# Loads of q and v put behind a product's copy on GpSimd, and the first weights and products of an attention-and-MoE kernel set in another order

## The chip, the cores and the metric

The kernel runs on one core of a Trainium2 chip. The metric is the device time of one launch in microseconds (us), lower is better. Engines are named as the profile names them: PE is TensorE's matrix unit, DVE is VectorE, ACT is ScalarE, POOL is GpSimd, and SP is SyncE, which here only issues DMAs.

## The reference

The program chains three layers. The MoE weights are stored in 64-bit floats, which the kernel reads as pairs of 32-bit words.

```python
# attention: q, k, v are 4 x 8 x 768 x 64; mem_k, mem_v are 4 x 8 x 8 x 64
for c in range(nc):                       # 24 chunks of 32 queries
    l_start = max(0, c_start - 16); r_end = min(S, c_end + 8)
    k_full = concatenate([mem_k, k[:, :, l_start:r_end]], axis=2)
    v_full = concatenate([mem_v, v[:, :, l_start:r_end]], axis=2)
    scores = matmul(q_c, k_full.T) / sqrt(64)
    a = exp(scores - max(scores)); a = a / (sum(a) + 1e-09)
    out[:, :, c_start:c_end] = matmul(a, v_full)
x = out.transpose(0, 2, 1, 3).reshape(3072, 512)
# MoE 1
h = x @ w_in                              # 512 x 2048
x = (h * tanh(log1p(exp(h)))) @ w_out     # 2048 x 512
# MoE 2
h = x @ w2_in
return (h / (1 + exp(-1.702 * h))) @ w2_out
```

## The kernel before, in words

The 3072 tokens are cut into 8 blocks of 384 (`TB`). Attention of a block works on four pairs of heads (hp 0 to 3). The first product of MoE 1 (x times w_in) for a block is 16 products, one for each 128 columns of w_in; they are numbered f0 to f15 within a block and `i = 16 j + f` over the program. All of them are `forward(j, f)`, whose matmuls stand on line 1166. In block 0 a product is 4 plain float32 matmuls, one for each pair of heads' 128 rows of x; from block 1 on it is 12 matmuls on high and low parts. Attention of block j+1 is woven between the products of block j: its scores (L1003), transposes of the exponentials (L1045) and values (L1065) on PE, its maxima (L1018), norms (L1037) and the transposes of loaded q (L679) and k (L682) on DVE, its exponentials (L1025) on ACT. It comes in two sets of two pairs of heads per block. Block 0's own attention stands ahead of everything and has its own code: exponentials L877, norms L896 and L904, transposes L923, values L940, copies of x L975 and L977. The layers behind (the second product of MoE 1 and both of MoE 2) run from about 370 us on and are not touched.

Each product's result leaves PSUM by a copy on ACT (L1298) or DVE (L1299) into a tile `z`, `gl` or `ev`, and goes from there to DRAM.

A tile W of w_in (W0 to W15, one per product) is loaded as 512 KB of 64-bit words by SP and converted in four steps: a drop (L423 on ACT; it could also be DVE), a shift (L432), a low part (L436) and a sign (L440) on DVE. From block 1 on the products use high and low parts made of it (L536 on ACT, L541 on DVE).

The order on each engine is not written by hand. Every operation is handed to a planner (`Plan`) with a rank, its engine's cost and the buffers that it reads and writes; `issue()` goes through them with assumed costs and lags and sets one static order per engine, in which each engine then runs. A buffer made by `fixed()` has no tile behind it: an operation that reads it is placed behind the writer in the plan, and no semaphore comes of it on the chip. Three such buffers matter here. `pace[i]` is written by product i. `opened` is written by a POOL copy of one element of block 0's values (`junk`, L1115), behind which v of block 1 is issued. `passed(j, i)` returns `pace[i]` for blocks from 2 on, so that loads of q and k stand `AHEADK` = 8 product ranks and those of v `AHEADV` = 4 ranks behind in the plan alone.

`load` (L382) issues DMAs: on SP, or on POOL when `via` is set. Loads of q of blocks 2 on and of v of blocks 1 on go through POOL; k always through SP. POOL and SP work through their queues in order, so a DMA issue that has to wait holds those behind it.

```python
load(rank - (LEAD if j == 1 and hp < 2 else 4), ql, qs, P * TB * 4, 128, passed(j, rank - AHEADK), via=NARROW * (j > 1))
load(rank, vt, parts, P * NCH * D * 4, 256, opened if j == 1 else passed(j, rank - AHEADV), via=NARROW)
```

Of the kernel before, what the change touches and what calls it, by code (L numbers as in the profile page):

```python
# [9 lines left out]
F32 = mybir.dt.float32  # L10
# [5 lines left out]
DRAM = bass.MemoryType.DRAM  # L16

NEG = -3.0e38
WARM = 11
NARROW = 0.64  # L20
WIDE = 0.95
# [1 line left out]
HELD = 4  # L23
LEAD = -1
AHEADW = 8
AHEADV = 4
SOON = 4
AHEAD = 6
CUT = 6
# [42 lines left out]
def fixed(t=None):  # L72

    b = Buf(None, None, None)
    b.tile = t
    return b
# [234 lines left out]
def kernel(  # L311
# [139 lines left out]
    def w_first(f):  # L451
        if f % 2 == 0:
            pairs.append(T[f"wo{f // 2}"].new([P, 2 * DM], F32))
        wi[f] = Part(pairs[-1], f % 2 * DM, DM)
        w_conv(1, f, 0, f - 1.5, (), wi[f], f"wi{f}")

    def w_cut(f):
        v = wi[f]
# [141 lines left out]
            tensor=src.tensor, offset=src.offset + r0 * D + col, ap=[[st * D, n] for st, n in dims] + [[1, width]]  # L600
        )

    x0, mem_t, pace, started, opened = {}, {}, {}, [], []

    class Inputs:

# [37 lines left out]
    def passed(j, i):  # L644
        return [pace[i]] if j > 1 and i >= 0 else []

    def pair_of_heads(j, hp, rank):
        b, s0 = divmod(j * TB, S)
        ql = T["ql"].new([P, TB // 32, 32], F32)
        kl = T["kl"].new([P, NKB, 32], F32)  # L650
        qT = T["qT"].new([P, 2 * (GQ + P)], F32)
        kT = T["kT"].new([P, NKB, BLK], F32)
        qs, ks = [], []
        for hh in range(2):
            for e in range(2):
                p0 = (2 * hh + e) * 32
                r0 = (b * H + 2 * hp + hh) * S + s0
                qs.append(lambda p0=p0, r0=r0, e=e: (
                    ql[p0:p0 + 32], rows(q, r0, [(1, 32), (32, TB // 32)], e * 32, 32)
                ))  # L660

                parts = [(0, 32, 0, NKB, -LEFT)]
                if r0 == 0:
                    parts = [
                        (0, 32, 1, NKB - 1, 32 - LEFT), (LEFT, 32 - LEFT, 0, 1, 0), (0, LEFT, 0, 1, 0)
                    ]
                elif r0 + TB == B * H * S:
                    parts = [
                        (0, 32, 0, NKB - 1, -LEFT), (0, LEFT, NKB - 1, 1, TB - LEFT),
                        (LEFT, 32 - LEFT, NKB - 1, 1, TB - LEFT),  # L670
                    ]
                for row, n, c, nb, t in parts:
                    ks.append(lambda row=row, n=n, c=c, nb=nb, t=t, p0=p0, r0=r0, e=e: (
                        kl[p0 + row:p0 + row + n, c:c + nb, :],
                        rows(k, r0 + t, [(1, n), (32, nb)], e * 32, 32),
                    ))
        load(rank - (LEAD if j == 1 and hp < 2 else 4), ql, qs, P * TB * 4, 128, passed(j, rank - AHEADK), via=NARROW * (j > 1))
        load(rank - (LEAD if j == 1 and hp < 2 else 4), kl, ks, P * NKB * 128, 128, passed(j, rank - AHEADK))
        add(rank, [("dve", dve(TB), lambda: nc.vector.transpose(  # L679
            out=qT[:, :TB], in_=ql.get().rearrange("p c d -> p (c d)")  # L680
        ))], reads=[ql], writes=[qT])
        add(rank, [("dve", dve(NKB * CHUNK), lambda: nc.vector.transpose(out=kT[:, :, :CHUNK], in_=kl.get()))], reads=[kl], writes=[kT])  # L682
        whole = fixed()

        def memory(eng):
            eng.tensor_copy(
                out=kT[:, :NCH, CHUNK:],
                in_=mem_t[b][:, hp, 0:NM].unsqueeze(1).to_broadcast([P, NCH, NM]),
            )

        add(
            rank,
            [("dve", dve(NCH * NM), lambda: memory(nc.vector)), ("pool", 0.3, lambda: memory(nc.gpsimd))],
            reads=[mem_t[b], kT], writes=[whole],
        )
        return qT, kT, whole

    def values_of(j, h0, rank):

        b, s0 = divmod(j * TB, S)  # L700
        vt = T["vh"].new([P, NCH, D], F32)
        parts = []
        for i in range(2):
            h = b * H + h0 + 2 * i
            t = h * S + s0 - LEFT
            runs = [(0, CHUNK, t, 0, NCH), (BLK, KEYS - BLK, t + CHUNK, 0, NCH)]
            if (h + 1) * S == B * H * S and s0 + TB == S:
                runs[1:] = [
                    (BLK, KEYS - BLK, t + CHUNK, 0, NCH - 1), (BLK, LEFT, t + TB, NCH - 1, 1),
                    (BLK + LEFT, RIGHT, t + TB, NCH - 1, 1),  # L710
                ]
            for row, n, r0, c, many in runs:
                parts.append(lambda row=i * D + row, n=n, r0=r0, c=c, many=many: (
                    vt[row:row + n, c:c + many], rows(v, r0, [(1, n), (CHUNK, many)], 0, D)
                ))
            if s0 == 0 or j == 1:
                parts.append(lambda row=i * D + CHUNK, h=h: (
                    vt[row:row + NM], rows(mem_v, h * NM, [(1, NM), (0, NCH)], 0, D)
                ))
        load(rank, vt, parts, P * NCH * D * 4, 256, opened if j == 1 else passed(j, rank - AHEADV), via=NARROW)  # L720
        return vt

    def first_values(gp, rank):
# [188 lines left out]
    def quad_out(j, hp, gp, vt, rank, names, e):  # L912
# [56 lines left out]
        for hh in range(1 if apart else 2):  # L969
            part = fixed()  # L970

            def hi(eng, hh=hh):
                x, y = cut(hh, x0[j][0])
                if eng == "act":
                    nc.scalar.activation(out=x, in_=y, func=AF.Copy)  # L975
                else:
                    nc.vector.tensor_copy(out=x, in_=y)  # L977

            def lo(hh=hh):
                x, y = cut(hh, x0[j][1])  # L980
                nc.vector.tensor_tensor(out=x, in0=y, in1=cut(hh, x0[j][0])[0], op=ALU.subtract)

            add(
                rank + 3.4,
                [("act", act(2 * GQ, True), lambda hi=hi: hi("act")), ("dve", dve(2 * GQ), lambda hi=hi: hi("dve"))],
                reads=[o], writes=[x0[j][0].buf(hp), part],
            )
            if j:
                add(rank + 3.6, [("dve", dve(2 * GQ), lo)], reads=[o, part], writes=[x0[j][1].buf(hp)])

    def duo(j, hp0, heads, r0):
# [82 lines left out]
        for i in range(2):  # L1074
# [7 lines left out]
                out=xl.at(hp), in0=o[i].get(), in1=xh.at(hp), op=ALU.subtract))],  # L1082
                reads=[o[i], part], writes=[xl.buf(hp)])

    def quads():

        last, todo = None, []
# [63 lines left out]
    def forward(j, f):  # L1151
# [17 lines left out]
                    n += 1  # L1169

        pace[i] = fixed()
        grain = KD // 2 if j else KD
        for k0 in range(0, KD, grain):
            kks = range(k0, k0 + grain)
            done = [pace[i]] if k0 + grain == KD else []
            add(
                i, [("pe", grain * (3 * 0.174 if j else 0.644), lambda kks=kks: go(kks))],
                reads=[*xs, *ws1], writes=[*done, h],
            )
        if j == 0:  # L1180
            w_cut(f)
        t = T[("gh", "gl", "ev")[i % 3] if j else ("gh", "gl")[f % 2]].new([P, TB], F32)
        copy(i + 0.3 - (URGENT if j else 0), View(t), h)
        (s, th), (fh, p) = divmod(j, 2), divmod(f, NP)
        key = 1, s, 2 * th + fh, p
        gds[key] = fixed()
        load(i + 0.4, gds[key], [lambda: (g1d[2 * th + fh][:, p, s * TB:(s + 1) * TB], t.get())], P * TB * 4, 1536, [t])
# [483 lines left out]
```

## Time and profile before

| what | value |
|---|---|
| median of 3 timed runs | 1097.83 us (1097.22 to 1099.79) |
| time of the profiled execution | 1095.65 us |
| its span in the profile | 1093.9 us |
| TensorE's mean granted clock in it | 0.990 of full speed |
| busy share of the span: PE, DVE, ACT, POOL | 98%, 73%, 49%, 15% |

The first row is what the kernel is judged by. The others come from one execution that was recorded by the profiler; the 1.75 us between its time and its span lie outside what the trace shows. A busy share is a mean over the whole span, and the stretches of the program differ widely: the first 42 us, in which block 0's attention runs, hold nearly all of the time in which PE stands idle.

### The profile page before, as it was taken

What the parts mean: (1) busy time and instruction counts of PE and PEld (TensorE: products, weight loads), DVE (VectorE), ACT (ScalarE), POOL (GpSimd) and SP (SyncE); (2) the same over time, 40 slices, a digit from 0 to 9 for tenths busy, and PEclk for the clock granted to TensorE, in tenths of its full rate; (3) what the DMA queues carried; (4) which work ended last, traced back from release to release, by engine and by line L of the source; (5) the groups of instructions that cost most, each with busy time, mean ns of one, the idle gap of its engine ahead of it and who ended that gap; (6) DMA issues with size and microseconds to landing.
All of it is one profiled execution on the core that took longest, in us unless ns stands there. A gap on an engine that the chain in (4) does not pass through costs nothing.

```text
span 1093.9 us, 25367 instructions
## 1 busy us (share of the span) xinstructions
PE 1075.9 (98%) x9936; PEld 1039.9 (95%) x9936; DVE 799.5 (73%) x1430; ACT 539.3 (49%) x1209; POOL 163.9 (15%) x273
## 2 busy tenths in 40 slices
PE   6899999999999999999999999999999999999998
PEld 5568999999999999999999999999999999999998
DVE  4896566766677689889869867666657877877875
ACT  4763544544545354555454656565565533323332
POOL 5339347537500000000000000000000000000000
PEclk8799999999999999999999999999999999999999
DMA  9998989989988573573453776868678545355361
GB/s 182 225 249 214 256 256 265 211 244 275 251 268 277 182 233 117 181 245 123 160 173 100 223 251 226 297 216 291 217 256 268 155 121 160 107 146 139 103 167 46
DMA packets 238800, 220.83 MB, mean 202 GB/s; under 512 B 70105, under 2 KB 211997, under 8 KB 238681
## 3 DMA queue, kind: packets, MB, share of 16 engines
q1 hardware_dynamic: 227865, 202.22, 62.6%
q0 software_dynamic: 9984, 16.21, 6.8%
q8 instruction: 78, 1.28, 0.5%
q10 hardware_dynamic: 832, 0.79, 0.3%
q14 instruction: 41, 0.34, 0.1%
HBM read 137.85 MB, written 81.26 MB: 200 GB/s over the span
## 4 chain that ended last, share of the span: by engine, by line
PE 90%; DMA 5%; DVE 4%; issue 1%; ACT 0%; SPq 0%; DVEq 0%; ACTq 0%
PE o L1166 12%; PE h L1166 12%; PE h L1328 9%; PE o L1429 9%; PE o L1521 9%; PE o L1328 8%; PE h L1429 6%; PE s L1429 6%; PE h L1521 6%; PE s L1521 5%; PE s L1328 4%; PE s L1065 1%; DMA wo<-in_q_dram 1%; DMA wi<-in_moe_w_in_dram 1%; PE s L1003 1%
## 5 line engine op out<-in xcount | busy, mean ns | idle before, releaser
L1166 PE MATMUL h<-xh,wi 128*128 128x384 f32 x320 | 83.7, 343 | 0.0
L1166 PE MATMUL o<-xh,wi 128*128 128x384 f32 x320 | 82.8, 340 | 0.0
L1166 PEld LDWEIGHTS o<-xh,wi 128*128 128x128 f32 x320 | 57.1, 188 | 0.6
L1166 PEld LDWEIGHTS h<-xh,wi 128*128 128x128 f32 x320 | 56.9, 188 | 0.6
L1166 PE MATMUL h<-xl,wi 128*128 128x384 f32 x160 | 53.9, 337 | 0.0
L1166 PE MATMUL o<-xl,wi 128*128 128x384 f32 x160 | 53.8, 336 | 0.0
L382 POOL DMA_DIRECT2D vt<-in_v_dram x62 | 41.0, 666 | 30.8 <-PE o L940 14.0
L1298 ACT ACTIVATE e<-h 128x384 f32<-128x384 f32 (+2 forms) x47 | 22.4, 477 | 45.5 <-PE h L1521 28.5
L1511 DVE TENSOR_TENSOR xl<-vt,xh 128x1024 fp32r<-128x1024 f32 x24 | 29.4, 1223 | 20.1 <-ACT xh L1508 18.0
L1521 PE MATMUL o<-wo,xh 128*128 128x256 f32 x232 | 43.7, 282 | 0.0
L1511 DVE TENSOR_TENSOR xl<-wi,xh 128x1024 fp32r<-128x1024 f32 x32 | 38.8, 1221 | 6.6 <-ACT xh L1508 5.9
L1429 PE MATMUL o<-xh,wo 128*128 128x256 f32 x224 | 40.7, 282 | 0.0
L382 POOL DMA_DIRECT2D wo<-in_q_dram x48 | 30.4, 639 | 45.7 <-DMA g1d<-z 16.9
L382 POOL DMA_DIRECT2D wo<-in_v_dram x56 | 35.9, 646 | 5.4 <-DMA wo<-in_q_dram 2.1
L1412 DVE TENSOR_TENSOR xl<-z,xh 128x1024 fp32r<-128x1024 f32 x24 | 29.2, 1223 | 10.2 <-ACT xh L1408 9.4
L1166 PE MATMUL h<-wo,wi 128*128 128x384 f32 x192 | 36.2, 341 | 0.0
L1521 PEld LDWEIGHTS o<-wo,xh 128*128 128x128 f32 x232 | 35.8, 190 | 0.0
L1166 PE MATMUL o<-wo,wi 128*128 128x384 f32 x192 | 35.8, 340 | 0.0
L1508 ACT ACTIVATE xh<-wi 128x1024 fp32r<-128x1024 f32 x25 | 26.4, 1054 | 18.5 <-DMA wi<-gd 8.9
L1298 ACT ACTIVATE ev<-o 128x384 f32<-128x384 f32 (+2 forms) x31 | 14.6, 471 | 42.1 <-PE o L1521 17.9
L1429 PEld LDWEIGHTS o<-xh,wo 128*128 128x128 f32 x224 | 34.8, 191 | 0.0
L1025 ACT ACTIVATE e<-s,mx 128x64 f32<-128x64 f32 x84 | 25.1, 319 | 18.1 <-DVE mx L1020 18.1
(442 smaller groups left out, 3538.8 us busy)
## 6 DMA issues: line engine op xcount, KB each, us to landing
st<-in_moe_w_out_dram SPq DMA_DIRECT2D x32, 512.0 KB
st<-wd SPq DMA_DIRECT2D x29, 512.0 KB
z<-g1d SPq DMA_DIRECT2D x24, 512.0 KB
vt<-gd SPq DMA_DIRECT2D x24, 512.0 KB
wi<-gd SPq DMA_DIRECT2D x24, 512.0 KB
g1d<-gl SPq DMA_DIRECT2D x46, 192.0 KB
g1d<-z SPq DMA_DIRECT2D x45, 192.0 KB
wi<-in_moe_w_in_dram SPq DMA_DIRECT2D x16, 512.0 KB
```

What stands on the lines that cost most here:

```text
L382: queue.dma_start(out=o, in_=i)
L1003: nc.tensor.matmul(out=s[hh][c0:c0 + CHUNK, g, i], lhsT=qT[d, c * CHUNK:(c + 1) * CHUNK], rhs=keys[d, c * BLK:c * BLK + KEYS], start=True, ...
L1025: nc.scalar.activation(out=e[:, g, i], in_=s[hh][:, g, i], func=AF.Exp, scale=scale, bias=mx[:, g, i:i + 1], accum_out=sm[:, g, i:i + 1],)
L1065: nc.tensor.matmul(out=o[i][hh * D:(hh + 1) * D, cs], lhsT=vt[hh][d, c], rhs=aT[hh][d, cs], start=True, stop=True, tile_position=(i * D, h ...
L1166: nc.tensor.matmul(out=h.get(), lhsT=a[:, c], rhs=b.at(kk), start=(n == 0), stop=(n == KD * len(prods) - 1))
L1298: ("act", act(n, True), lambda: nc.scalar.activation(out=dst(), in_=bank.get(), func=AF.Copy)),
L1328: nc.tensor.matmul(out=bank.get(), lhsT=a, rhs=b, start=(fresh and m == 0), stop=(m == 3 * K2 - 1), skip_group_check=not fresh,)
L1412: add(rank + 0.05, [("dve", dve(n2), lambda gh=gh, gl=gl, src=src: nc.vector.tensor_tensor(out=flat(gl), in0=flat(src), in1=flat(gh), op=A ...
L1429: nc.tensor.matmul(out=bank[:, d, :], lhsT=a, rhs=b[:, p, :], start=(fresh and h == d == p == m == 0), stop=(h == 1 and p == HP - 1 and m ...
L1508: ("act", act(NP * P), lambda: nc.scalar.activation(out=flat(gh), in_=flat(src), func=AF.Copy)),
L1511: add(rank + 0.05, [("dve", dve(NP * P), lambda: nc.vector.tensor_tensor(out=flat(gl), in0=flat(src), in1=flat(gh), op=ALU.subtract))], re ...
L1521: nc.tensor.matmul(out=bank.get(), lhsT=a[:, p], rhs=b, start=(fresh and p == 0 and m == 0), stop=(p == NP - 1 and m == 2), skip_group_che ...
```

## The change

Three edits. First, a product's copy becomes a gate: for twelve sets of attention (two per block, blocks 2 to 7), POOL copies one element of the tile that holds the copy of a given product into `mark`, and the loads of q (product 5 ahead of the set's base) and of v (3 ahead) are placed behind such a copy on POOL. The copy reads a tile, so it waits for the product's copy on the chip, and what stands behind it in POOL's queue waits too. Loads of k keep `passed`. Second, the conversions of W0 and W1 (`w_first`) read `opened`, that is, they are planned behind the arrival of block 0's values. Third, `SPLIT` = 2: products f0 and f1 of block 0 are handed to the planner as four operations of one matmul each, where an operation reads the part of x of its own pair of heads (`fresh`) rather than all of x; only the last one reads all.

```diff
+SPLIT = 2
...
-AHEADV = 4
+AHEADQ = 5
+AHEADV = 3
...
-        w_conv(1, f, 0, f - 1.5, (), wi[f], f"wi{f}")
+        w_conv(1, f, 0, f - 1.5, opened if f < 2 else (), wi[f], f"wi{f}")
...
-    x0, mem_t, pace, started, opened = {}, {}, {}, [], []
+    x0, mem_t, pace, started, opened, fresh = {}, {}, {}, [], [], {}
...
+    def gate(j, i):
+        return [gates[i]] if j > 1 else []
...
-        load(rank - (LEAD if j == 1 and hp < 2 else 4), ql, qs, P * TB * 4, 128, passed(j, rank - AHEADK), via=NARROW * (j > 1))
+        load(rank - (LEAD if j == 1 and hp < 2 else 4), ql, qs, P * TB * 4, 128, gate(j, rank - AHEADQ), via=NARROW * (j > 1))
...
-        load(rank, vt, parts, P * NCH * D * 4, 256, opened if j == 1 else passed(j, rank - AHEADV), via=NARROW)
+        load(rank, vt, parts, P * NCH * D * 4, 256, opened if j == 1 else gate(j, rank - AHEADV), via=NARROW)
...
+            if j == 0:
+                fresh.setdefault(hp, []).append(part)
...
+    gates = {}
+    mark = sb.tile([P, 1], F32, name="mark")
+    STEPS = [NF * (j - 1) - SOON + 8 * n for j in range(2, NB) for n in range(2)]
...
-        grain = KD // 2 if j else KD
+        grain = KD // 2 if j else 1 if f < SPLIT else KD
...
-                reads=[*xs, *ws1], writes=[*done, h],
+                reads=[*(xs if j or done else fresh[k0]), *ws1], writes=[*done, h],
...
+        if i + AHEADQ in STEPS or i + AHEADV in STEPS:
+            gates[i] = fixed()
+            add(i + 0.6, [("pool", 0.15, lambda: nc.gpsimd.tensor_copy(out=mark[:1], in_=t[:1, :1]))], reads=[t], writes=[gates[i]])
```

What the planner makes of it is shown at four places. Numbers behind names tell buffers and tiles apart; lines of the changed kernel are 2 to 14 higher than those of before.

On ACT, the stretch behind the first exponentials of block 0 (`e` and `ev` 96x128) before; `wo0_291<-wi0_118` is the drop of W0, `wo0_291<-wi1_120` that of W1:

```order
L877 ACTIVATE e_207,sm_231<-e_207,mx_208 96x128 x4
L877 ACTIVATE ev_225,sm_260<-ev_225,mx_226 96x128 x4
L423 ACTIVATE wo0_291<-wi0_118 128x512
L877 ACTIVATE e_274,sm_294<-e_274,mx_275 96x128 x4
L929 ACTIVATE z3_325<-o2_318 128x384
L877 ACTIVATE ev_310,sm_329<-ev_310,mx_311 96x128 x3
L975 ACTIVATE xh_348<-o3_332 128x192
L877 ACTIVATE ev_310,sm_329<-ev_310,mx_311 96x128
L806 ACTIVATE wi11_149<-h_296 128x120 x2
L423 ACTIVATE wo0_291<-wi1_120 128x512
```

and in the changed kernel, where the drop of W0 stands at the fifth place behind these rows and that of W1 seven rows further:

```order
L882 ACTIVATE e_208,sm_232<-e_208,mx_209 96x128 x4
L882 ACTIVATE ev_226,sm_261<-ev_226,mx_227 96x128 x4
L909 ACTIVATE e_208<-e_208,r_266 96x128 x4
L882 ACTIVATE e_275,sm_315<-e_275,mx_276 96x128 x4
L882 ACTIVATE ev_296,sm_342<-ev_296,mx_297 96x128 x4
L811 ACTIVATE wi11_150<-h_302 128x120 x2
L980 ACTIVATE xh_378<-o3_352 128x192
L882 ACTIVATE e_347,sm_381<-e_347,mx_348 96x128 x3
L934 ACTIVATE z3_331<-o2_390 128x384
L882 ACTIVATE e_347,sm_381<-e_347,mx_348 96x128
L882 ACTIVATE ev_386,sm_410<-ev_386,mx_387 96x128 x2
L934 ACTIVATE z3_331<-o2_414 128x384
```

The drop of W0 has moved from right behind the first eight exponentials to behind the second pair of heads' and most of the third's.

On PE, the end of block 0's attention and the first products before (`z,vt` are values, `ident,e` and `ident,ev` transposes, `xh,wo` the products; f0 and f1 are the two `h` rows of four matmuls):

```order
L940 MATMUL o3_593<-z3_325,vt_128 64x96 x4
L923 MATMUL o2_615<-ident_64,e_449 128x96 x4
L940 MATMUL o3_633<-z3_325,vt_107 64x96 x4
L923 MATMUL o2_645<-ident_64,ev_481 128x96 x4
L940 MATMUL o3_662<-z3_325,vt_128 64x96 x4
L1166 MATMUL h_685<-xh_348,wo0_291 128x384 x4
L1045 MATMUL s1_715<-ident_64,e_640 128x128 x3
L1166 MATMUL h_719<-xh_348,wo0_291 128x384 x4
L1045 MATMUL o1_740<-ident_64,e_677 128x128 x3
L1166 MATMUL o2_746<-xh_348,wo1_613 128x384 x4
```

and in the changed kernel:

```order
L928 MATMUL o2_576<-ident_64,ev_386 128x96 x4
L1177 MATMUL h_594<-xh_378,wo0_475 128x384
L945 MATMUL o3_600<-z3_331,vt_129 64x96 x4
L928 MATMUL o2_614<-ident_64,e_460 128x96 x4
L1177 MATMUL h_594<-xh_378,wo0_475 128x384 x2
L945 MATMUL o3_644<-z3_331,vt_108 64x96 x4
L928 MATMUL o2_655<-ident_64,ev_497 128x96 x4
L1177 MATMUL h_666<-xh_378,wo0_475 128x384
L945 MATMUL o3_674<-z3_331,vt_129 64x96 x4
L1177 MATMUL h_666<-xh_378,wo0_475 128x384
L1052 MATMUL s1_696<-ident_64,e_623 128x128 x3
L1177 MATMUL h_594<-xh_378,wo0_475 128x384
```

Four of the eight matmuls of f0 and f1 now stand between the last transposes and values of block 0, one of them ahead of the third last values.

On POOL, the place where q and v of block 2 are issued, behind the copies of memory keys for block 1, before:

```order
L686 COPY z1_756<-z0_137 128x12x8
L686 COPY wo15_422<-z0_137 128x12x8
L382 DMA z0_137<-in_q_dram 32x12x32 x4
L382 DMA wo12_402<-in_v_dram 32x12x64
L382 DMA wo12_402<-in_v_dram 24x12x64
L382 DMA wo12_402<-in_mem_v_dram 8x12x64
L382 DMA wo12_402<-in_v_dram 32x12x64
L382 DMA wo13_123<-in_q_dram 32x12x32 x4
```

and in the changed kernel:

```order
L691 COPY z1_762<-z0_138 128x12x8
L691 COPY wo15_431<-z0_138 128x12x8
L1198 COPY mark_65<-gl_1000 1x1
L384 DMA z0_138<-in_q_dram 32x12x32 x4
L384 DMA wo13_124<-in_q_dram 32x12x32 x4
L691 COPY z1_762<-z0_138 128x12x8
L1198 COPY mark_65<-gl_1071 1x1
L384 DMA wo12_407<-in_v_dram 32x12x64
L384 DMA wo12_407<-in_v_dram 24x12x64
```

Each group of loads now stands behind a `mark` copy, and both pairs of heads' q (eight DMAs) stand behind one.

On SP, the loads of W4 to W9 and of q and k of block 1's last two pairs of heads, before:

```order
L382 DMA wi5_249<-in_moe_w_in_dram 128x4x256
L382 DMA wi6_305<-in_moe_w_in_dram 128x4x256
L382 DMA wi7_376<-in_moe_w_in_dram 128x4x256
L382 DMA wo13_123<-in_q_dram 32x12x32 x4
L382 DMA wo13_123<-in_k_dram 32x13x32 x4
L382 DMA z0_137<-in_q_dram 32x12x32 x4
L382 DMA z0_137<-in_k_dram 32x13x32 x4
L382 DMA wi8_622<-in_moe_w_in_dram 128x4x256
L382 DMA wi9_627<-in_moe_w_in_dram 128x4x256
```

and in the changed kernel:

```order
L384 DMA wi4_246<-in_moe_w_in_dram 128x4x256
L384 DMA wi5_250<-in_moe_w_in_dram 128x4x256
L384 DMA wo13_124<-in_q_dram 32x12x32 x4
L384 DMA wo13_124<-in_k_dram 32x13x32 x4
L384 DMA z0_138<-in_q_dram 32x12x32 x4
L384 DMA z0_138<-in_k_dram 32x13x32 x4
L384 DMA wi6_619<-in_moe_w_in_dram 128x4x256
L384 DMA wi7_627<-in_moe_w_in_dram 128x4x256
L384 DMA wi8_634<-in_moe_w_in_dram 128x4x256
```

W6 and W7 (the last two of six loads of W before) have moved behind q and k of these pairs of heads.

## Rows read from the trace of the kernel before

**Rows 1.** Busy time by stretches (us, then instructions), TensorE's granted clock, DMA share.

```profile
core 0: us, PE busy (x) PEld busy (x) DVE busy (x) ACT busy (x) POOL busy (x), PEclk, DMA share, GB/s
35.10:45.30 10.20, 8.75 (x124) 5.87 (x101) 9.70 (x30) 10.20 (x44) 5.05 (x8) 0.50 1.12 241
71.56:93.04 21.48, 21.48 (x254) 13.45 (x255) 20.05 (x46) 11.40 (x38) 16.86 (x27) 1.00 0.85 202
93.04:366.00 272.96, 272.96 (x3600) 264.74 (x3599) 174.64 (x440) 129.86 (x442) 118.02 (x193) 1.00 0.92 253
```

**Rows 2.** TensorE in order of time: start, us, what, idle before it and its releaser.

```profile
22.14 0.91 PE L940 MATMUL o<-z,vt 128*64 128x96 f32 x8 [4.16 <-POOL wo L686]
...
41.16 0.91 PE L940 MATMUL o<-z,vt 128*64 128x96 f32 x8 [0.65 <-DVE z L930]
42.00 4.47 PE L1166 MATMUL h<-xh,wo 128*128 128x384 f32 x8
...
46.63 2.75 PE L1166 MATMUL h<-xh,wo 128*128 128x384 f32 x8
...
49.54 5.33 PE L1166 MATMUL o<-xh,wo 128*128 128x384 f32 x16
...
68.12 2.74 PE L1166 MATMUL h<-xh,wo 128*128 128x384 f32 x8
...
71.56 0.52 PE L1045 MATMUL s<-ident,e 128*128 128x128 f32 x3 [0.70 <-DVE e L1037]
...
93.04 0.81 PE L1166 MATMUL h<-xh,wi 128*128 128x384 f32 x2
...
108.39 0.24 PE L1003 MATMUL s<-wo 64*32 64x64 f32 x1
```

**Rows 3.** ScalarE in order of time.

```profile
19.46 0.66 ACT L423 ACTIVATE wo<-wi 128x512 f32<-128x512 f32 x1 [5.20 <-DMA wi<-in_moe_w_in_dram]
...
55.26 0.70 ACT L423 ACTIVATE wo<-wi 128x512 f32<-128x512 f32 x1 [3.21 <-DMA wi<-in_moe_w_in_dram]
...
56.77 0.69 ACT L423 ACTIVATE wo<-wi 128x512 f32<-128x512 f32 x1 [0.43 <-DMA wi<-in_moe_w_in_dram]
...
106.38 0.49 ACT L1298 ACTIVATE ev<-h 128x384 f32<-128x384 f32 x1 [1.75 <-PE h L1166]
```

**Rows 4.** VectorE in order of time.

```profile
33.40 0.56 DVE L682 STREAM_TRANSPOSE wo<-z 128x416 f32<-128x416 f32 x1
...
54.54 0.83 DVE L432 TENSOR_SCALAR wo<-wo 128x512 int32<-128x512 int32 x2
...
60.80 0.56 DVE L1081 TENSOR_TENSOR xl<-o,xh 128x384 fp32r<-128x384 f32 x1 [0.48 <-ACT xh L1077]
...
69.33 0.67 DVE L436 SCALAR_TENSOR_TENSOR wo<-wi,wo 128x512 int32<-128x512 int32 x1
...
70.01 0.41 DVE L432 TENSOR_SCALAR wo<-wo 128x512 int32<-128x512 int32 x1
...
70.44 0.50 DVE L1299 COPY z<-o 128x384 f32<-128x384 f32 x1
70.88 0.54 DVE L1037 TENSOR_TENSOR e<-e,r 128x384 f32<-128x384 f32 x1
```

**Rows 5.** SyncE's DMA issues in order of time.

```profile
28.56 5.68 SPq L382 DMA_DIRECT2D wi<-in_moe_w_in_dram  x6
...
48.84 1.28 SPq L382 DMA_DIRECT2D wi<-in_moe_w_in_dram  x2
```

**Rows 6.** GpSimd in order of time.

```profile
18.01 0.18 POOL L1115 COPY junk<-vt 1x1 f32<-1x1 f32 x1 [9.63 <-DMA vt<-in_v_dram]
```

**Rows 7.** Loads of q, 100 to 300 us: ns min/median/max of an issue, then time to landing.

```profile
L382 POOL DMA_DIRECT2D wo<-in_q_dram x40: 615/617/881, 101.8 to 290.0; - x40
...
DMA to landing us min/median/max: 2.3/4.7/8.2
```

**Rows 8.** Loads of v, the same stretch.

```profile
DMA to landing us min/median/max: 2.6/5.5/9.3
```

## The prediction

> **What bounds the kernel now.** I read the busy shares first, then time by stretches, then the engines in order of time around the places that the change touches. TensorE is busy for 98% of the span. From 71.56 us to 366 us, blocks 0 to 7, it is busy for the whole of each stretch, while VectorE is busy for 20.05 of 21.48 us up to 93.04 us and for 174.64 of 272.96 us after that [rows 1]. So from 71.56 us on an edit to loads can only cost time; what the change can gain lies before. There TensorE waits 4.16 us for the first values, 0.65 us for the last, and 0.70 us at 71.56 us, where the transposes of block 1's exponentials wait for VectorE's norm [rows 2]. [...]
>
> The reader should see a relay. ScalarE stands for 5.20 us at the drop of W0, whose load is not there [rows 3], with the second pair of heads' exponentials queued behind it. TensorE then does block 0's last values at 41.16 us, f0 at 42.00 and f2 from 49.54 us [rows 2]. But what ends last at 71.56 us is VectorE: it goes from W6's shift at 54.54 us to the norm at 70.88 us with a single wait shown, 0.48 us [rows 4]. A TensorE that gets there sooner waits longer for that norm, unless VectorE gets there sooner too.
>
> **The opening, worked out.** *W0 and W1 later.* ScalarE no longer stands 5.20 us at W0 [rows 3], so exponentials and the first values come about 3 to 4 us sooner; the values were there at 18.01 us, when GpSimd's copy of them ran [rows 6]. I count this as almost nothing by itself: the new order on VectorE has the transposes of block 1's first two pairs of heads ahead of the maxima of block 0's last pair, and those loads arrive when they did. They were there at 33.40 us at the latest [rows 4]. From that row to the last values is 7.76 us before, 0.65 of it idle on TensorE. In the new order VectorE has three more instructions of the sizes 0.41 to 0.67 us [rows 4] and four short ones in that stretch, 1.5 to 2.2 us. So the last values start at most at 33.40 + 7.76 - 0.65 + 2.2 = 42.7 us; if the load was there 1.5 us sooner, at 41.2 us, where they stood.
>
> *Pair by pair.* Four of the eight matmuls of f0 and f1 then lie behind TensorE. After the last values (0.91 us) there remain four, 2.75 us at full and 4.47 us at half clock, and some 0.35 us of transposes. f2 starts between 41.2 + 0.9 + 2.75 + 0.35 = 45.2 us and 42.7 + 0.9 + 4.47 + 0.35 = 48.4 us, against 49.54: 1.1 to 4.3 us sooner. f8 ended at 68.12 + 2.74 = 70.86 us and would end at 66.5 to 69.7 us.
>
> *VectorE's side.* The six loads of W on SyncE took 5.68 us to issue, 0.95 each, and W8 was issued from 48.84 us [rows 5]. W6 and W7 now stand behind q and k, which so start 1.9 us sooner; W7 is issued at 47.9 us. W8 was there 6.42 us behind its issue, at 55.26 us, and W9 1.51 us later [rows 3]. So W7 is there between 55.26 - 1.51 = 53.75 us and 47.9 + 6.42 = 54.3 us, and after its drop of 0.70 us its shift can run at 54.5 to 55.1 us, against 54.54 before. From there to the norm the new order has three instructions fewer on VectorE: one low part (0.67), one shift (0.41) and one copy (0.50) [rows 4]. That is 1.58 us, and about 1.4 us with the overlap by which each starts before its predecessor's row ends. The wait of 0.48 us at 60.80 us goes as well, since ScalarE's copy before it is due sooner. That makes 1.9 us less 0 to 0.6 us. If W7 came at 52.8 us, a spacing of W earlier, it would be 2.9 us. I take 1.9 us: the spacing of loads is the nearer row, since the queue is never empty there.
>
> *What is kept.* The transposes at 71.56 us start 1.9 us sooner, and TensorE is there (at least 1.86 us sooner). The three instructions now come behind the norm: VectorE's work up to the end of block 0 grows from 20.05 to about 21.45 us, in a stretch of 21.48 us. It just fits.
>
> **The gates.** Twenty-four copies of one element on GpSimd, 0.18 us each by the like one [rows 6], cost 4.3 us of an engine with time to spare. What they cost is the wait: before, q of a block was issued when its buffer was free, long ahead. Now a set's eight loads of q stand behind product 5 ahead of the set's base. Queued behind them on GpSimd are the copies of memory keys and v; behind the late q stand VectorE's transposes of q and, in order, product copies and conversions, and TensorE's scores wait for these. Take the set behind f15 of block 0: f15 ends at 93.04 us and its set's scores start at 108.39 us [rows 2], a window of 15.35 us. In it go: the copy (it starts right behind the product and takes 0.49 us [rows 3]), with 1.0 us allowed; the mark, 0.2 us; eight issues at 0.617 us, 4.9 us; landing, 4.7 us in the middle and 8.2 us at most [rows 7]; one transpose, 0.6 us (VectorE's row for k [rows 4]). Sum 11.4 us, at worst 14.9 us. It fits in all twelve sets, so I cost it at 0 us; VectorE stands idle meanwhile, which its 98 us of spare time covers. If that cover is gone, each us late is a us on TensorE. v is gated two products later and lands in 5.5 us, at most 9.3 us [rows 8]; its values follow the scores by a softmax, so q is late first.
>
> [...] An issue of q took 0.617 us in the middle and 0.881 us at most, with VectorE busy 64% of that time [rows 1, 7]; eight at the longest would be 7.0 us, and the sum of the middle 13.5 us, still inside. [...]
>
> **Sum.** 1095.65 us for the profiled execution less 1.9 us is 1093.75 us. That execution lay 2.18 us under the median of the runs shown, so on the median it is 1097.83 - 1.9 = 1095.9 us. About 0.2%, 2.2 us, is what a measurement of this kernel can tell from no change, and the forecast lies just inside.
>
> **Rivals.**
> *More.* W7 comes early and TensorE's 1.1 to 4.3 us all tell: the norm is ready 2.9 to 3.7 us sooner, 1094.1 to 1094.9 us. For it: the loads of q and v of block 2 have left the DMA engines of that time. Against it: the stretch that follows has no spare VectorE time to hold so much.
> *Nothing.* VectorE meets one wait of a us or two between the norm and the end of block 0, where its work now fills the stretch, and TensorE waits where it was never waiting; or the landings push the last values past 43 us at half clock. The gain shrinks to 0 to 0.8 us: 1097.0 to 1097.8 us. For it: 21.45 of 21.48 us. Against it: some of that work is conversions that no product needs until block 1.
> *Slower: q behind its gate.* ScalarE's copy of the gate product can stand behind twelve exponentials, or q can land at its longest, and VectorE, held at the transposes, owes a backlog. TensorE loses time in a set once copy and landing together pass 15.35 - 0.2 - 4.9 - 0.6 = 9.6 us; the rows give 5.7 in the middle and 9.2 at most. With 1 us lost in five of twelve sets the sum is 1095.9 + 5 = 1100.9 us.
>
> **How the numbers follow.** Forecast (gain 1.3 to 2.8 us, 1095.0 to 1096.5 us) 0.50; more 0.18; nothing 0.15; slower 0.16; the locked port 0.01. I predict 1095.9 us. The range goes from 1093.0 us (the larger gain and a us for the spread of medians) to 1101.0 us (q late in five sets). Faster by over 0.2% is below 1095.6 us: all of "more" and about half of the forecast's range, 0.42; slower is q late and the lock, 0.16; the rest, 0.42.
>
> **What would show it.** Right: ScalarE's wait of 5.20 us gone; first values near 19 us; four matmuls of f0 and f1 ahead of the last values; the shift of W6 and W7 still near 54.5 us; the transposes at 71.56 us near 69.7 us; no TensorE wait from there to 366 us, with VectorE waiting for q behind the marks. Wrong: a TensorE wait between 70 and 93 us (the gain given back), waits at scores (L1010 in the changed kernel) or at product banks in blocks 1 to 7 (q too late), or W7 far from 54 us.

## The result, and the profile after

| | median | runs | profiled execution: time, span |
|---|---|---|---|
| before, beside the changed kernel | 1097.53 us | 4 (1095.79 to 1099.79) | 1095.65 us, 1093.9 us |
| changed | 1109.28 us | 4 (1106.61 to 1111.69) | 1111.69 us, 1109.9 us |

The change makes the kernel slower: the ratio is 1.0105, with an interval of 1.0072 to 1.0139. I had predicted 1095.9 us and a range up to 1101.0 us. The profiled execution of the changed kernel is the longest of its four, so the trace holds 16.0 us of difference in span where the medians differ by 11.75 us.

**The opening's gain came out at the forecast size.** TensorE in order of time, in the changed kernel, beside [rows 2]:

```profile
18.59 0.55 PE L945 MATMUL o<-z,vt 128*64 128x96 f32 x8
...
43.22 0.55 PE L945 MATMUL o<-z,vt 128*64 128x96 f32 x8
...
46.71 2.74 PE L1177 MATMUL o<-xh,wo 128*128 128x384 f32 x8
...
69.58 0.52 PE L1052 MATMUL s<-ident,e 128*128 128x128 f32 x3 [0.80 <-ACT wo L425]
```

The first values come 3.55 us sooner, f2 starts at 46.71 instead of 49.54 us, and the transposes of block 1's exponentials stand at 69.58 instead of 71.56 us. VectorE, beside [rows 4]:

```profile
27.89 0.61 DVE L687 STREAM_TRANSPOSE wo<-wo 128x416 f32<-128x416 f32 x1 [3.52 <-DMA wo<-in_k_dram]
31.15 0.58 DVE L684 STREAM_TRANSPOSE wo<-z 128x384 f32<-128x384 f32 x1 [2.65 <-DMA z<-in_q_dram]
...
52.63 0.71 DVE L434 TENSOR_SCALAR wo<-wo 128x512 int32<-128x512 int32 x2
...
57.01 0.56 DVE L1088 TENSOR_TENSOR xl<-s,xh 128x384 fp32r<-128x384 f32 x1 [2.00 <-ACT xh L1084]
...
68.89 0.54 DVE L1044 TENSOR_TENSOR e<-e,r 128x384 f32<-128x384 f32 x1
```

Before, VectorE stood for a load of k right ahead of the shift of W6 and W7 at 54.54 us:

```profile
54.00 0.61 DVE L682 STREAM_TRANSPOSE wo<-z 128x416 f32<-128x416 f32 x1 [1.69 <-DMA z<-in_k_dram]
```

ScalarE's wait of 5.20 us at W0 [rows 3] is gone; the longest at a drop is now this one, and block 1's high part, for which VectorE waits 2.00 us, stands behind it:

```profile
55.93 0.67 ACT L425 ACTIVATE wo<-wi 128x512 f32<-128x512 f32 x1 [2.38 <-DMA wi<-in_moe_w_in_dram]
56.50 0.48 ACT L1084 ACTIVATE xh<-s 128x384 fp32r<-128x384 f32 x1
```

**The loss lies in blocks 1 to 7.** I cut both spans where block 1's first product starts (91.13 us in the changed kernel; the cut stands 0.03 us ahead of it) and where the same number of TensorE's instructions is left. Before and after, busy time by stretches (columns as in [rows 1]):

```profile
93.04:370.66 277.62, 277.62 (x3626) 269.40 (x3625) 176.88 (x444) 130.85 (x444) 118.02 (x193) 1.00 0.92 252
370.66:1093.90 723.24, 717.99 (x5379) 715.39 (x5378) 548.84 (x739) 351.71 (x560) 0.00 (x0) 1.00 0.58 181
```

```profile
69.58:91.10 21.52, 21.52 (x253) 13.50 (x254) 21.04 (x49) 11.88 (x38) 17.40 (x23) 1.00 0.85 196
91.10:384.00 292.90, 282.58 (x3627) 273.84 (x3626) 177.30 (x445) 129.66 (x444) 130.86 (x227) 0.98 0.86 241
384.00:1109.90 725.90, 718.33 (x5379) 715.32 (x5378) 549.37 (x739) 352.13 (x560) 0.00 (x0) 1.00 0.58 180
```

So block 1 begins 93.04 - 91.10 = 1.94 us sooner, and then 292.90 - 277.62 = 15.28 us are lost in blocks 1 to 7 and 2.66 us behind them: -1.94 + 15.28 + 2.66 = 16.0 us. Of the 15.28 us, TensorE is idle for 10.32 us and busy 4.96 us longer for the same work. The waits of that idle time, changed kernel, 72 to 370 us:

```profile
engine line waited for: us in total, times, longest us
PE s L1010 <- issue: 9.5, 3, 4.4
PE h L1177 <- issue: 0.7, 1, 0.7
```

The same view of the kernel before has no row. "Issue" says that the engine waited for nothing that the profile shows. The chain of waits puts one of the long ones in the middle of a set's scores:

```profile
190.31 0.04 PE o L1010
190.34 4.41 issue
194.75 0.21 PE s L1010
```

Most of the busy time that is longer is half clock behind such waits:

```profile
190.34:194.75 4.41, 0.00 (x1) 0.00 (x1) 0.74 (x2) 0.00 (x0) 0.08 (x1) 1.00 1.19 208
194.75:198.00 3.25, 3.25 (x36) 3.16 (x36) 1.35 (x6) 0.51 (x2) 0.00 (x0) 0.55 0.20 35
280.68:284.89 4.21, 0.00 (x0) 0.00 (x0) 1.29 (x3) 0.23 (x1) 0.00 (x0) 0.87 1.08 330
284.89:290.00 5.11, 5.11 (x84) 4.93 (x84) 1.35 (x6) 2.18 (x14) 0.00 (x0) 0.50 0.53 120
```

After 4.41 us of idle TensorE the granted clock is 0.55, and after 4.21 us it is 0.50. By these rows the two stretches cost 3.25 x 0.45 + 5.11 x 0.50 = 4.0 of the 4.96 us (an estimate: busy time times the missing share of the clock). A late q is not the cause of the wait at 190.34 us: the set's two transposes of q on VectorE ran without a wait before the scores began at 189.4 us:

```profile
186.73 0.56 DVE L684 STREAM_TRANSPOSE z<-wo 128x384 f32<-128x384 f32 x1
...
187.80 0.56 DVE L684 STREAM_TRANSPOSE wo<-z 128x384 f32<-128x384 f32 x1
```

### The profile page after: what moved, and what is told of

The parts are those of the page before. It is cut to its first block, busy times and chain, and to the rows that moved or that the text cites. A ratio compares the mean times of both kernels' runs of the same rounds, so it can differ in the third digit from the quotient of the medians.

```text
span 1109.9 us, 25386 instructions
## 1 busy us (share of the span) xinstructions
PE 1077.9 (97%) x9936; PEld 1041.6 (94%) x9936; DVE 799.2 (72%) x1431; ACT 539.2 (49%) x1212; POOL 172.8 (16%) x296
## 3 DMA queue, kind: packets, MB, share of 16 engines
q8 instruction: 78, 1.28, 0.5%
## 4 chain that ended last, share of the span: by engine, by line
PE 87%; DMA 6%; DVE 3%; issue 2%; ACT 1%; SPq 0%; DVEq 0%; ACTq 0%
PE o L1177 12%; PE h L1177 12%; PE o L1443 9%; PE o L1535 9%; PE h L1342 8%; PE o L1342 7%; PE s L1443 6%; PE h L1443 6%; PE h L1535 6%; PE s L1535 5%; PE s L1342 4%; PE s L1072 1%; DMA wo<-in_q_dram 1%; DMA wi<-in_moe_w_in_dram 1%; PE s L1010 1%
## 5 line engine op out<-in xcount | busy, mean ns | idle before, releaser
L1525 DVE TENSOR_TENSOR xl<-vt,xh 128x1024 fp32r<-128x1024 f32 x24 | 29.4, 1223 | 19.9 <-ACT xh L1522 17.8
L1535 PE MATMUL o<-wo,xh 128*128 128x256 f32 x232 | 43.7, 282 | 0.0
L1525 DVE TENSOR_TENSOR xl<-wi,xh 128x1024 fp32r<-128x1024 f32 x32 | 38.8, 1222 | 5.9 <-ACT xh L1522 5.0
L1177 PE MATMUL o<-wo,wi 128*128 128x384 f32 x192 | 38.1, 353 | 0.0
L1535 PEld LDWEIGHTS o<-wo,xh 128*128 128x128 f32 x232 | 35.8, 190 | 0.0
L1177 PEld LDWEIGHTS o<-wo,wi 128*128 128x128 f32 x192 | 34.7, 197 | 0.4 <-issue 0.2
L1177 PEld LDWEIGHTS h<-wo,wi 128*128 128x128 f32 x192 | 33.7, 190 | 0.1
```

The lines of the kernel that those rows point to most:

```text
L1177: nc.tensor.matmul(out=h.get(), lhsT=a[:, c], rhs=b.at(kk), start=(n == 0), stop=(n == KD * len(prods) - 1))
L1525: add(rank + 0.05, [("dve", dve(NP * P), lambda: nc.vector.tensor_tensor(out=flat(gl), in0=flat(src), in1=flat(gh), op=ALU.subtract))], re ...
L1535: nc.tensor.matmul(out=bank.get(), lhsT=a[:, p], rhs=b, start=(fresh and p == 0 and m == 0), stop=(p == NP - 1 and m == 2), skip_group_che ...
```

## The experiments

Ratios are to the kernel before, run on the same chip as the experiment; that median was 1097.98 us for the first four, 1099.38 us for the next four and 1098.34 us for the last three. They are the ratios on record with their 95% intervals; the quotient of two medians differs from them by up to 0.0014. The "issue" waits are those of one profiled execution each.

| run | what it has | median us | ratio (interval) | "issue" waits, us (72 to 384) |
|---|---|---|---|---|
| e1_opening | opening edits alone | 1099.14 | 1.0006 (0.9988 to 1.0025) | none |
| e2_gates | gates alone | 1107.78 | 1.0099 (1.0061 to 1.0137) | 6.2 |
| e3_plan | gates in the plan, not on the chip | 1102.33 | 1.0026 (1.0004 to 1.0049) | 3.8 |
| e4_lead8 | gates 3 and 1 products earlier | 1099.44 | 1.0010 (0.9994 to 1.0026) | 1.2 |
| e5_q | only q gated | 1105.85 | 1.0069 (1.0050 to 1.0089) | 4.6 |
| e6_v | only v gated | 1098.09 | 0.9996 (0.9986 to 1.0006) | 1.0 |
| e7_shift | 16 small matmuls at the start | 1106.16, one run | | 5.4 |
| e8_block2 | gates for block 2 alone | 1095.51 | 0.9967 (0.9956 to 0.9979) | none |
| e9_adjacent | e8, values moved next to scores | 1101.37 | 1.0032 (1.0011 to 1.0054) | 4.2 |
| e10_lead4 | q's gate one product later | 1107.51 | 1.0095 (1.0075 to 1.0115) | 2.4 |
| e11_apart | six matmuls put between | 1104.68 | 1.0062 (1.0033 to 1.0090) | 2.9 |

**Which half of the change, and the plan or the wait.** `e1_opening` takes the gates out, `e2_gates` the opening edits, `e3_plan` leaves the order that the gates make in the plan but puts no semaphore and no `mark` on the chip, `e4_lead8` moves the gates.

```diff
# e1_opening (and no mark copies)
-AHEADV = 3
+AHEADV = 4
-    ... gate(j, rank - AHEADQ), via=NARROW * (j > 1))
+    ... passed(j, rank - AHEADK), via=NARROW * (j > 1))
-    ... opened if j == 1 else gate(j, rank - AHEADV), via=NARROW)
+    ... opened if j == 1 else passed(j, rank - AHEADV), via=NARROW)
# e2_gates
-SPLIT = 2
+SPLIT = 0
-        w_conv(1, f, 0, f - 1.5, opened if f < 2 else (), wi[f], f"wi{f}")
+        w_conv(1, f, 0, f - 1.5, (), wi[f], f"wi{f}")
# e3_plan (and no mark copies)
-    ... gate(j, rank - AHEADQ)      ... gate(j, rank - AHEADV)
+    ... passed(j, rank - AHEADQ)    ... passed(j, rank - AHEADV)
# e4_lead8
-AHEADQ = 5
-AHEADV = 3
+AHEADQ = 8
+AHEADV = 4
```

> The two edits of the opening alone (W0's and W1's conversions behind block 0's values, f0 and f1 pair by pair); q and v as in the kernel before. Theory A (the loss lies in the gates: q and v are loaded at the same time as k around the scores, and TensorE's own instructions, which come by DMA too, arrive late behind them): the opening's 1.9 us remain as a gain, about 1095.6 us against 1097.5, no wait of TensorE without a releaser at the scores, block 1's first product near 91.1 us. Theory B (the new order of the opening does harm later, by a shifted phase of all loads): 1100 us or more.

> The gates alone, the opening as before. Theory A: 1097.5 + 11.8 + 1.9 = about 1111 us, with TensorE waits of 1 to 5 us in the middle of scores (L1010 or its like) that no engine releases. Theory B: within 2 us of 1097.5.

> The whole change, but q and v wait for the product in the plan alone (the same leads of 5 and 3 products, no copy into mark, so no wait on the chip). Theory A, where the real wait makes q and v late and bunches them with k: about 1096 us and no such TensorE waits, since GpSimd issues when buffers are free. Theory C (the planned leads alone, through where they put transposes and other instructions on VectorE, make the loss): 1106 us or more.

> The whole change with longer leads: q behind the product 8 ahead of the set's base (not 5), v 4 ahead (not 3); the waits are real. Each product ahead is about 2.2 to 2.5 us. Theory D (q itself comes late for the scores, as the slower rival had it): 7 us more for q, all waits at scores gone, about 1095.6 us. Theory A: q leaves the time of the scores but v still meets k there; part of the loss stays, 1098 to 1106 us.

The gates alone cost what the whole change costs: 1.0099 beside 1.0105. With the same gates at 8 and 4 products instead of 5 and 3 nothing is lost that a measurement can tell. The plan without any wait on the chip costs a part, and has one "issue" wait of 3.8 us. Its 1102.33 us lie between the two forecasts for it (about 1096, and 1106 or more), so it decides for neither. So the loss hangs on the lead, and at least a part of it on the order alone.

The opening edits alone bring nothing either, which I had not forecast, and `e4_lead8` at 1.0010 is not the 1095.6 us of theory D: it has lost the gain too. In `e1_opening` the transposes that stand at 69.58 us in the changed kernel come at 73.14 us, since VectorE is held for a buffer that is still being stored (TensorE, then VectorE, in order of time):

```profile
73.14 0.52 PE L1052 MATMUL s<-ident,e 128*128 128x128 f32 x3 [3.87 <-DVE e L1044]
```

```profile
70.29 0.56 DVE L1310 COPY z<-o 128x384 f32<-128x384 f32 x1 [3.58 <-DMA g1d<-z]
```

At 60 to 72 us GpSimd issues four loads of block 2's values there, and none in the changed kernel. The gates of block 2 are what keeps the opening's gain: `e8_block2`, below, has the opening edits and no other gates, and keeps it. That these loads are what holds the store is argued, not shown.

**Which gate.** `e5_q` gates q alone (v at 4 products, in the plan alone), `e6_v` gates v alone (q at 8).

```diff
# e5_q
-AHEADV = 3
+AHEADV = 4
-    ... opened if j == 1 else gate(j, rank - AHEADV), via=NARROW)
+    ... opened if j == 1 else passed(j, rank - AHEADV), via=NARROW)
-        if i + AHEADQ in STEPS or i + AHEADV in STEPS:
+        if i + AHEADQ in STEPS:
# e6_v
-    ... gate(j, rank - AHEADQ), via=NARROW * (j > 1))
+    ... passed(j, rank - AHEADK), via=NARROW * (j > 1))
-        if i + AHEADQ in STEPS or i + AHEADV in STEPS:
+        if i + AHEADV in STEPS:
```

> The whole change, but v is not gated: it waits in the plan alone, 4 products ahead, as before; q keeps its gate of 5 products. Theory A1 (v, gated late, meets the next set's k in the ten us ahead of the scores and delays TensorE's instruction loads): most of the loss is gone, 1097 to 1101 us, TensorE waits without a releaser under 3 us in all. Theory A2 (q's gate makes it, since k shares q's buffers and comes late behind it): 1105 us or more.

> The whole change, but q is not gated: it waits in the plan alone, 8 products ahead, as before; v keeps its gate of 3 products. Theory A1: 1105 us or more, with TensorE waits without a releaser at the scores. Theory A2: 1097 to 1101 us.

It is q's gate: 1.0069 against 0.9996. The times are those of theory A2, but its reason, a k that comes late behind q, is not what the waits below show. The waits of `e5_q` have again no releaser, and the longest lies at 191.25 us, where the changed kernel had its own at 190.34 us:

```profile
PE o L1072 <- issue: 3.1, 1, 3.1
PE o L1010 <- issue: 1.2, 1, 1.2
```

**What TensorE waits for.** The page has a DMA queue of instructions; of the changed kernel (packets, MB, share of 16 engines):

```profile
q8 instruction: 78, 1.28, 0.5%
```

1.28 MB in 78 packets is 16 KB a packet. TensorE runs 9936 matmuls and 9936 weight loads, 19872 / 78 = 254.8 to a packet if the queue is TensorE's alone. Count what TensorE had done at the start of each "issue" wait (changed kernel):

```profile
0.00:190.34 190.34, 176.23 (x2359) 148.22 (x2360) 132.92 (x404) 100.36 (x368) 102.25 (x174) 0.97 0.93 232
0.00:215.35 215.35, 196.83 (x2611) 168.01 (x2612) 147.47 (x441) 111.05 (x407) 113.55 (x193) 0.97 0.91 225
0.00:235.08 235.08, 215.64 (x2864) 186.06 (x2864) 160.03 (x476) 119.18 (x440) 123.85 (x211) 0.97 0.90 225
0.00:280.68 280.68, 260.50 (x3496) 229.36 (x3497) 186.63 (x546) 138.35 (x513) 150.49 (x257) 0.98 0.91 230
```

Matmuls and loads together are 4719, 5223, 5728 and 6993: apart by 504, 505 and 1265, which is 2, 2 and 5 times 252 to 253, about what one packet has. So I read the waits as standing at the borders of pieces that a packet brings. During the first of them, from 192.00 to 192.50 us, one packet of that queue moves, among 248 others (the same columns, over 0.5 us):

```profile
q0 software_dynamic: 61, 0.09, 80.7%
q1 hardware_dynamic: 187, 0.02, 38.3%
q8 instruction: 1, 0.02, 14.4%
```

From 190.34 to 192.00 us that queue moves nothing. `e7_shift` puts 16 tiny matmuls at the start of the program (32 matmuls and 32 loads in the count). If the wait belongs to an instruction of the program, a semaphore that the profile doesn't show, it stays at that instruction; if it belongs to a piece, it moves 64 instructions up the program and stays at the count.

```diff
             nc.tensor.matmul(out=spare.get(), lhsT=ident.get(), rhs=ident.get(), start=True, stop=True)
+        for _ in range(16):
+            nc.tensor.matmul(out=spare.get()[:32, :8], lhsT=ident.get()[:, :32], rhs=ident.get()[:, :8], start=True, stop=True)
```

> The whole change with 16 tiny matmuls more on TensorE at the very start, which are 64 instructions by the profile's way of counting (each matmul is two weight loads and two matmuls there); nothing else moves. [...] Theory E (a score waits for a semaphore that the profile doesn't name, for q, k or a buffer): the wait stands at the same matmul as in the changed kernel.

```profile
0.00:191.13 191.13, 177.90 (x2360) 149.26 (x2360) 132.64 (x403) 101.31 (x368) 98.69 (x172) 0.96 0.95 231
0.00:232.47 232.47, 215.19 (x2864) 185.25 (x2864) 157.00 (x469) 119.21 (x438) 119.28 (x207) 0.96 0.90 223
0.00:286.23 286.23, 268.56 (x3624) 236.94 (x3625) 190.75 (x560) 141.82 (x527) 149.57 (x260) 0.96 0.92 232
```

The long wait (4.05 us, from 191.13 us) stands at 4720 of the count, as in the changed kernel (4719), and so 31 score matmuls earlier in the program. Of the set's 96 score records, the changed kernel had 69 behind it (24 + 24 below, and 11 + 10 of the second pair of heads); `e7_shift` had 38 (the line's groups, up to the wait). The 32 matmuls that stand ahead would shift it by 32 if it keeps to the count, and it shifted by 31. Changed kernel, then `e7_shift`:

```profile
L1010 PE MATMUL s<-z x24: 212/216/240, 189.4 to 189.9; 64*32 64x64 f32 x24
L1010 PE MATMUL o<-z x24: 216/216/240, 189.4 to 189.9; 64*32 64x64 f32 x24
```

```profile
L1010 PE MATMUL s<-z x20: 213/216/240, 190.5 to 190.9; 64*32 64x64 f32 x20
L1010 PE MATMUL o<-z x18: 216/216/240, 190.5 to 190.9; 64*32 64x64 f32 x18
```

The wait keeps to the count, so I read it as TensorE out of instructions; a semaphore that the profile doesn't name would have held the same matmul in both, as theory E had it. The border near 6993, where the changed kernel lost 4.21 us, cost `e7_shift` nothing: it has no "issue" wait between 232.47 and 286.23 us.

**Why there.** All kernels have 78 such packets, and so some 78 borders; few cost anything. What differs is TensorE's order. Where q is gated at 5 products the plan puts off one set's scores and then sets the next set's values directly ahead of the next scores (order on TensorE in the changed kernel; the values of block 4's first set and the scores of its second):

```order
1020 L1177 MATMUL o_2775<-xh,wi_865 128x384 x2
1021 L1177 MATMUL o_2775<-xl,wi_865 128x384
1022 L1072 MATMUL s_2787<-z_331,wo_407 64x32
...
1069 L1072 MATMUL o_2789<-z_331,wo_407 64x32
1070 L1010 MATMUL s_2839<-z_762 32x64
1071 L1010 MATMUL o_2841<-z_762 32x64
```

These are 48 values and 48 scores with no product between them. Before, 24 to 30 product matmuls stand there from block 1 on. The pattern stands in two places in the changed kernel and in `e2_gates`, in one in `e3_plan`, as scores ahead of values once in `e5_q`, and nowhere in the kernel before, in `e1_opening`, `e4_lead8`, `e6_v` and `e8_block2`: just the kernels with 1.2 us of "issue" waits at most.

The traces also hold when each packet of the queue moved. Take the piece between the counts 4467 and 4719, busy time by stretches, before and in the changed kernel:

```profile
185.39:191.08 5.69, 5.69 (x140) 5.40 (x137) 3.64 (x8) 2.00 (x4) 3.72 (x7) 1.00 0.95 267
188.41:190.34 1.93, 1.93 (x142) 1.74 (x135) 0.76 (x2) 0.49 (x1) 1.16 (x2) 1.00 1.12 244
```

Before, the piece takes TensorE 5.69 us, and the next packet lands 3.85 us after TensorE enters it; in the changed kernel the piece takes 1.93 us, and the packet lands after 4.98 us. In all thirteen kernels that packet lands 2.8 to 5.4 us after TensorE enters the piece. In `e9_adjacent`, below, it lands after 3.79 us, about as before, but the piece is done in 1.87 us, and TensorE stands 3.6 us.

`e8_block2` keeps the gates of block 2, which the opening needs, and no others. `e9_adjacent` puts the pattern back into it by the rank of two sets' values and adds no load, no gate and no wait. `e10_lead4` and `e11_apart` keep all gates, and have six product matmuls between values and scores at the closest place.

```diff
# e8_block2 (STEPS for block 2 alone)
-        return [gates[i]] if j > 1 else []
+        return [gates[i]] if j == 2 else []
-    ... gate(j, rank - AHEADQ), via=NARROW * (j > 1))
+    ... (gate(j, rank - AHEADQ) if j == 2 else passed(j, rank - AHEADK)), via=NARROW * (j > 1))
-    ... opened if j == 1 else gate(j, rank - AHEADV), via=NARROW)
+    ... opened if j == 1 else gate(j, rank - AHEADV) if j == 2 else passed(j, rank - 4), via=NARROW)
# e9_adjacent, on e8_block2
-        add(r0 + VAL, [("pe", COSTV, values)], reads=[*vt, *aT], writes=o)
+        add(r0 + VAL + 2.2 * (j in (4, 6) and hp0 == 0), [("pe", COSTV, values)], reads=[*vt, *aT], writes=o)
# e10_lead4
-AHEADQ = 5
+AHEADQ = 4
# e11_apart
-        add(r0 + SCORE, [("pe", COSTS, scores)], reads=reads, writes=s)
+        add(r0 + SCORE + 1 * (j in (4, 6) and hp0 == 2), [("pe", COSTS, scores)], reads=reads, writes=s)
```

> The opening's edits, and gates for block 2 alone: q and v of block 2 stay out of the opening's loads, those of blocks 3 to 7 wait in the plan alone, 8 and 4 products ahead, as before. Theory A: the 1.9 us of the opening are kept and the waits at later scores are gone: about 1095.6 us against 1097.5 for the kernel before. Theory F (the gain of the opening does not reach the end in any arrangement): 1097.5 us or more.

> e8 (the opening's edits, gates for block 2 alone), with one thing put back from the changed kernel's order by another way: in two sets, in blocks 4 and 6, the values get a rank 2.2 products later, so that TensorE does 48 values and the next set's 48 scores with no product between them; loads and gates as in e8. Theory R (such a row of short matmuls uses up TensorE's instructions faster than they are loaded): a wait without a releaser of 2 to 4.5 us in or near the two rows, with some half clock behind it; 1100 to 1106 us where e8 gave 1095.5. Theory G (late or bunched loads of q and v behind real gates make the wait): no gate and no load is later than in e8, so 1095.5 us and no such wait.

> The whole change with q's gate one product closer (4 ahead, not 5). In this order no values stand directly before scores (6 matmuls are between them at the closest place). Theory G: q comes 2.2 us later and the loss grows, 1110 us or more. Theory R: the two waits of over 4 us are gone or under 2 us each, 1097 to 1104 us; waits for q itself may show at some scores.

> The whole change, gates and leads as they are, but the scores of the two sets that stood directly behind values (blocks 4 and 6, second pairs) get a rank 1 later, which puts 6 matmuls of a product between. That half product takes about 1.0 us and needs few instructions. Theory R: the waits of 4.4 and 4.2 us shrink by about 1 us each, 1104 to 1108 us. Theory G: 1109 us, the waits as they were.

`e8_block2` beats both kernels: 1095.51 us, 0.9967 (0.9956 to 0.9979), with the transposes at 69.46 us, block 1 at 91.04 us and no "issue" wait from 72 us on. `e9_adjacent` is 5.86 us slower than it, though on another chip; its ratio's interval lies clear of that of `e8_block2`. Its waits, 72 to 384 us:

```profile
PE o L1010 <- issue: 3.6, 1, 3.6
PE s L1010 <- issue: 0.6, 1, 0.6
```

The first stands at 2358 matmuls and 2358 loads, the border where the changed kernel waited. So the order alone makes such a wait, with no gate of a later block in the kernel. The second place with the pattern cost only the 0.6 us.

`e10_lead4` at 1107.51 us met neither forecast (1097 to 1104, and 1110 or more): six matmuls between did not bring the time back. Its "issue" waits are down to 2.4 us, but TensorE now waits for the softmax, which I read as the price of a later q:

```profile
PE s L1052 <- DVE e L1044: 4.2, 2, 2.5
PE s L1010 <- issue: 2.0, 1, 2.0
PE s L1052 <- ACT wo L425: 1.3, 1, 1.3
```

`e11_apart` is slower than the kernel before; against the changed kernel, 1.0062 beside 1.0105, the intervals overlap, and its runs go from 1098.56 to 1110.93 us. Its profiled execution is the lowest of its ten and has 2.9 us of such waits; what the longer ones had, no trace shows. The median is in theory R's range, but six matmuls are no sure cure.

## Why the prediction was wrong, step by step

**The opening: the size right, the path not.** First values at 18.59 us ("near 19 us"), f2 at 46.71 us (45.2 to 48.4: that range has four matmuls at 2.75 and at 4.47 us, which before ran at a granted clock of 1.00 and 0.63), transposes at 69.58 us (69.7), and block 1's first product 1.91 us sooner (1.9). VectorE's work did just fit: 21.04 of 21.52 us. But the 1.9 us were to come from three instructions fewer between the shift of W6 and W7 and the norm, with the shift still at 54.5 to 55.1 us. It ran at 52.63 us, and from there to the norm VectorE took 68.89 - 52.63 = 16.26 us, where before it took 16.34. What set the shift's time before was not W7's load but the wait of 1.69 us for k just ahead of it; SyncE now issues that k ahead of W6 and W7, and the wait is gone. W7 was early too: SyncE issued W6 at 44.28 us and W7 some 0.9 us later, not at 47.9, and ScalarE dropped W7 at 51.98 us. The gain that I had forecast, the fewer instructions, went into VectorE's 2.00 us for ScalarE's high part at 57.01 us. So the near hit at 69.58 us is luck: a gain that I had not seen stands in for the one that a wait took back. The releaser that the profile names there is a drop of W on ScalarE, not the norm. The last values came at 43.22 us, 0.5 us later than my latest, behind two late loads on VectorE, and f2 was still in its range, since part of the first two products' matmuls now lay ahead of them.

**The gates: the step that failed.** It reads: "It fits in all twelve sets, so I cost it at 0 us". The sum for one set held: q was there and transposed before its scores at 189.4 us, and GpSimd's issues did not lengthen (615 ns in the middle and 853 at most, beside [rows 7]):

```profile
L384 POOL DMA_DIRECT2D wo<-in_q_dram x36: 615/615/853, 115.4 to 296.1; - x36
```

What I left out is that a gate is also an edge in the plan. I costed it in the order of the kernel before, and the plan answers a later q with another order of scores and values on TensorE. That order, as I read it, ran TensorE's instructions dry: 10.2 us of waits, 8.6 of them at the two places where values stand directly ahead of scores, and 4.96 us more of busy time, most of it half clock behind them. In place of 0 us the step is worth +9.8 us by `e2_gates` (1107.78 - 1097.98).

**The rivals.** "Slower: q behind its gate" named the right part and the wrong mechanism. Its price of 5 us rested on late landings, which the long waits don't show; `e10_lead4`, one product later, is where late work begins to cost. The locked port, with 0.01 among the chances, is shown by no run: q's issues in the row above took 615 ns in the middle and 853 at most. "Nothing" failed, as the gain was kept up to 91 us. "More" had W7 early, and it was, but VectorE's wait for ScalarE took the rest.

**What would show it.** I had named waits at scores in blocks 1 to 7 as the sign of q too late. The waits came at the scores, and the releaser column told the cause apart: a late q would show VectorE's transpose, not "issue".

**What stays open.** Why a refill lands as late as it does, 2.8 to 5.4 us after TensorE enters a piece. From 182 to 192 us, up to where the packet moves, the changed kernel's DMA engines move 2627 packets, 1760 of them under 512 B; in a like stretch before (178 to 188 us) it is 2215 and 853. Loads in small packets may delay the refill; no run took them away at the same order. `e9_adjacent` shows the order to be enough, not that the traffic does nothing. The 2.66 us lost behind block 7 were not tried either; 2.1 us is one wait for VectorE (`PE s L1535`, for `xl` of L1525), where before had 0.4 us. Before, too, 5.25 us of TensorE's 18.0 idle us lie behind 370.66 us and 12.1 us in the first 42 us: two thirds, not nearly all as I had it at the start. And `e8_block2` gained 3.9 us on the medians where its opening explains some 2; its profiled span is 1.2 us under that of before.

## What to carry to other kernels

A dependency that a planner sees costs twice: the wait, and the order that it makes of everything else; lay the whole order of the bound engine beside the old one, above all where many short instructions come to stand together, before a wait is costed at zero. An idle engine with "issue" as its releaser deserves a count of its instructions up to each such wait: here the counts differed by multiples of one number, 252 to 253, and by that I read the engine as waiting for instructions, not data. Where a wait protects one stretch (here block 2's loads against the opening), put it there alone.

## What the runs showed of the hardware

In every kernel the DMA queue that the page calls "instruction" moved 1.28 MB in 78 packets, 16 KB each. The waits of the changed kernel stand 504, 505 and 1265 matmuls and weight loads of TensorE apart, multiples of 252 to 253, and 19872 / 78 is 254.8; so I read a packet as TensorE's next 252 to 255 instructions. At the border looked at above, the packet landed 2.8 to 5.4 us after TensorE entered the piece before: TensorE stood for 2.4 to 4.4 us where it ran that piece in 1.9 to 2.3 us (six kernels), for 1.2 and 2.0 us where it took 3.1 us (`e11_apart` and `e10_lead4`), and for 1.0 us at most where it took 5.7 to 5.9 us (five kernels). 48 values and 48 scores took from 187.83 to 190.34 us for 165 of their 192 records, 15 ns each beside its weight load, where the eight records of f2 took 2.74 us. Beside the 10.3 us of idle time stand 4.96 us of longer busy time, about half a us for each us, with the granted clock at 0.50 to 0.55 in the 3 to 5 us behind the two long ones.
